# Block-sparse attention and a cosine-routed expert layer on one core: first pair in half transfers, bf16 mask rows, routing sums on GpSimd, early dispatch in 16 steps, x and weights in pieces, PSUM pools of their own

## The chip, the cores and the metric

The kernel runs on one core of a Trainium2 chip. TensorE (PE) does the matmuls, with its weight loads shown as a row of their own (PEld); VectorE (DVE), ScalarE (ACT) and GpSimd (POOL) do the rest, and SyncE (SP) issues most transfers. The metric is the device time of one execution in microseconds, as the median of several. All times below are microseconds unless ns is written.

## The reference

```python
# attention: batch 4, heads 8, 768 tokens, 64 per head, blocks of 32 tokens
scores = scale * q @ k.T                      # per batch and head
mask = |blk_i - blk_j| <= 1, or block 0 or 23 on either side,
       or one of 3 sampled key blocks of the query's block
attn = exp(scores masked to -1e9, less the row's maximum) / (sum + 1e-9)
x = (attn @ v), heads side by side            # 3072 rows of 512
# experts: 8 of them, F = 1024, one per row
logits = normed(x) @ normed(expert_emb).T / tau
expert_idx = argmax(logits); gate = softmax(logits)[expert_idx]
out[row] = gate * (relu(x[row] @ w1[e]) @ w2[e])
```

## The kernel before, in words

**Attention.** Heads are handled in 16 pairs, four pairs to a sequence (a batch item). A pair has two halves of 384 queries, and a half has six key chunks of 128. One half and one chunk is a unit, `u`; 192 units in all, 6 to a half pair, 12 to a pair, 48 to a sequence. `score_fast` adds the mask and the scores of a unit in PSUM: four bf16 matmuls of `kmask` by `qmask` and eight f32 matmul passes of `kt` by `qt`, and ScalarE takes the exp into `e` (four buffers, L300). The mask is a product: `kmask` has a row for each block with ones at its tokens, `qmask` for each block the value (0 or -1e9) that it gives to a query. `attend_fast` multiplies with V into `av` (L318) and adds up `esum` on VectorE (L313, L315); after the sixth chunk ScalarE copies half of `av` out (L322) and VectorE adds the other (L324). `turn_fast` transposes K and Q of the next pair on PE (L280) and copies them out with VectorE (`kt`, L283) and ScalarE (`qt`, L284).

`settle` (called at u % 6 = 3 for the half pair before) turns the result back into rows (L346), sums the denominators (L353), and writes rows of x and parts of the logits (L361, L364). `squares` (u % 6 = 4) squares x and adds up its columns on GpSimd (L375, L379).

**Routing.** `after_sequence` makes a plan of steps for the units that follow a sequence: the four steps of `route` at units 8, 10, 11 and 13 (sum of squares, sum of logit parts, norm and argmax, gate, then x to DRAM), `rank` at 14 (three products on PE, then VectorE), and after the second sequence `dispatch_early` in nine steps at units 16 to 26, which finds five full tiles of 128 rows of one expert; then the transfers for expert tiles 0 and 1 at units 28 and 29 (`fetch`), and `prepare` of tile 0 at 44. x and the weights go in whole transfers of 1.5 MB and 2 MB.

**Experts.** `expert_tile` does 64 f32 matmul passes for the hidden layer in two halves of 32 (`hp`, L685), the transposes of the next tile (L670) and the second layer (`yp`, L698). At tile 0, between the halves, the last half pair is settled and the last sequence routed.

**Order.** The framework orders the instructions of each engine by program order and readiness: an instruction traced late but ready early may be moved forward. `issue_after(ins)` puts what is traced in its block behind `ins`, on that instruction's engine alone and without waiting for its end. Each engine then works in that fixed order. Pools of PSUM lie on a stack: `small` (one tile of two banks, for turn, settle, rank and others), `big_f` (two tiles of two banks, the scores), `acc` (two banks, av); after attention `eps` takes the six banks of the last two.

**Start.** `attention_fast` L726 to L742: ids and the first pair's K on SP and Q on ScalarE's queue, V, the expert table, the second pair, then constants, mask (`build_mask`), expert table, both halves of `turn_fast`, and two `score_fast`.

Of the kernel before, what the change touches and what calls it, by code (L numbers as in the profile page):

```python
# [11 lines left out]
F32 = mybir.dt.float32  # L12
# [45 lines left out]

def build_consts(k):
    nc, pool = k.nc, k.const  # L60
    k.ident = pool.tile([P, P], F32, name="ident")
    make_identity(nc, k.ident[:])
# [35 lines left out]
def build_mask(k):  # L98


    nc, pool = k.nc, k.setup
    ids_f = pool.tile([NB, NRAND], F32, name="ids_f")
    nc.vector.tensor_copy(out=ids_f, in_=k.ids)

# [6 lines left out]
    for val in (0.0, float(NB - 1)):  # L111
        for pos in (col, row):
            nc.vector.scalar_tensor_tensor(out=m, in0=pos, scalar=val, in1=m, op0=ALU.is_equal, op1=ALU.max)
# [3 lines left out]
    nc.vector.tensor_scalar(out=m, in0=m, scalar1=1.0, scalar2=-NEG, op0=ALU.subtract, op1=ALU.mult)  # L117

    oh = pool.tile([P, NC, NB], F32, name="oh_blk")
# [14 lines left out]
    if not k.exact:  # L134
        k.kmask = k.const.tile([P, S], BF16, name="kmask")
        k.qmask = k.const.tile([P, S], BF16, name="qmask")
        nc.gpsimd.memset(k.kmask, 0.0)
        nc.gpsimd.memset(k.qmask, 0.0)
        for h in range(2):
            nc.vector.tensor_copy(out=k.kmask[D * h:D * h + NB, :], in_=krow)  # L140
            nc.scalar.copy(out=k.qmask[D * h:D * h + NB, :], in_=qr[0:NB, 0:S])
        return
# [41 lines left out]
def load_pair(k, g, parts=(0, 1, 2), engine=None):  # L184
    b, j = g // NPAIR, g % NPAIR
    got = k.loaded.setdefault(g, [None, None, None])
    for i in parts:
# [6 lines left out]
        got[i] = t  # L194

# [71 lines left out]
def turn_fast(k, g, part):  # L267
# [6 lines left out]
    for n in range(2):  # L274
        src = k.loaded[g][n]
        for c in range(NQ):
            for r in range(2):
                toks = slice(D * r, D * (r + 1))
                for h in range(2):
                    nc.tensor.matmul(ps[D * h:D * (h + 1), r, n, c, :], lhsT=src[toks, h, part * NQ + c, :],  # L280
                                     rhs=k.ident[toks, toks], start=True, stop=True)
# [46 lines left out]
def settle(k, w):  # L328
# [28 lines left out]
    nc.vector.tensor_scalar(out=den, in0=den, scalar1=1e-9, scalar2=None, op0=ALU.add)  # L357
    inv = k.sp.tile([P, NQ, 2], F32, name="inv", tag="inv")
# [68 lines left out]
def route(k, b):  # L427
# [7 lines left out]
    else:  # L435
        nc.vector.reduce_sum(out=nrm, in_=k.nsq[b], axis=AX.X)
# [7 lines left out]
    if not k.exact:  # L444
        nc.vector.reduce_sum(out=l, in_=k.part[b].rearrange("p c h e -> p c e h"), axis=AX.X)
# [17 lines left out]
    gate = p.tile([P, NC], F32, name="gate")  # L463
    nc.vector.reduce_sum(out=gate, in_=ex, axis=AX.X)
    nc.vector.tensor_scalar(out=gate, in0=gate, scalar1=1e-9, scalar2=None, op0=ALU.add)
    nc.vector.reciprocal(out=x[:, :, DM:XW], in_=gate.unsqueeze(2))
    for dram in (k.x_early, k.x_dram):
        if dram is k.x_dram or b < EARLY:
            nc.sync.dma_start(out=dram[b * S:(b + 1) * S, :].rearrange("(p c) w -> p (c w)", c=NC),
                              in_=x.rearrange("p c w -> p (c w)"))  # L470
    for c in range(NC):
        t = b * NC + c
        nc.gpsimd.tensor_tensor(out=k.seen[:, t + 1, :], in0=k.seen[:, t, :], in1=k.oh[:, t, :], op=ALU.add)
    yield

# [17 lines left out]
def add_up(k, t):  # L493

    for step in (1, 2, 4):
# [3 lines left out]
        t = nxt  # L499
    return t  # L500


def tile_experts(k, end, tiles, name):
# [6 lines left out]
    nc.vector.reduce_sum(out=ex, in_=past, axis=AX.X)  # L510
    nc.vector.tensor_scalar(out=ex, in0=ex, scalar1=float(E - 1), scalar2=None, op0=ALU.min)
# [16 lines left out]
def split_places(k, pos, nt, tiles):  # L528
# [8 lines left out]
    nc.vector.scalar_tensor_tensor(out=low, in0=hi, scalar=-float(G), in1=pos, op0=ALU.mult, op1=ALU.add)  # L537
    nc.vector.tensor_tensor(out=ge[:, :, 0:tiles], in0=ge[:, :, 0:tiles], in1=ge[:, :, 1:tiles + 1], op=ALU.subtract)
# [31 lines left out]
def dispatch_early(k):  # L570
# [8 lines left out]
    end = add_up(k, full)  # L579
    yield  # L580
    nc.vector.tensor_scalar(out=end, in0=end, scalar1=float(NE), scalar2=None, op0=ALU.min)
    k.experts = [tile_experts(k, end, NE, "expert_e")]
# [6 lines left out]
    pos = of_expert(k, base, nt, "pos")  # L589
    late = p.tile([P, nt], F32, name="late")  # L590
    taken = of_expert(k, k.taken, nt, "taken_t")
    nc.vector.tensor_tensor(out=late, in0=k.rank[:, 0:nt], in1=taken, op=ALU.is_ge)
# [3 lines left out]
    low, val = split_places(k, pos, nt, NE)  # L596
# [6 lines left out]
def dispatch_late(k):  # L603
# [9 lines left out]
    end = add_up(k, need)  # L613
    k.used = k.const.tile([P, 1], I32, name="used")
    nc.vector.tensor_scalar(out=k.used, in0=end[:, E - 1:E], scalar1=float(NG), scalar2=None, op0=ALU.min)
    k.experts.append(tile_experts(k, end, NG, "expert_l"))
# [9 lines left out]
    low, val = split_places(k, pos, NT, NG)  # L626
# [15 lines left out]
def fetch(k, i):  # L642
    nc = k.nc
    late = int(i >= NE)
    t = i - NE if late else i
    e = nc.values_load(k.experts[late][0:1, t:t + 1], engines=(mybir.EngineType.SP,), min_val=0, max_val=E - 1)
    wp = k.wp if i % 3 < 2 else k.wp2
    w1 = ring(k, "w1", i, 3, wp, [P, ND, F])
    nc.sync.dma_start(out=w1, in_=k.w1[bass.ds(e, 1), :, :].rearrange("o (c p) f -> p (o c) f", p=P))
    w2 = ring(k, "w2", i, 3, wp, [P, NF, DM])  # L650
    nc.sync.dma_start(out=w2, in_=k.w2[bass.ds(e, 1), :, :].rearrange("o (c p) m -> p (o c) m", p=P))
    x = ring(k, "xg", i, 4, k.wp, [P, XW])
    slot = k.slots[late][:, t:t + 1]
    nc.gpsimd.indirect_dma_start(  # L654
# [4 lines left out]
    k.fetched[i] = (w1, w2, x, slot)  # L659
# [281 lines left out]
```

## Time and profile before

| | us |
|---|---|
| median of 3 runs (779.92 to 782.65) | 780.49 |
| the profiled execution | 785.54 |
| its span, first to last instruction | 783.6 |
| first attention matmul (L318) starts | 20.4 |
| last unit's attention matmul starts | 372.4 |
| first expert matmul (L685) starts | 374.68 |
| one expert tile in the steady stretch | 14.45 |
| mean granted clock | 0.992 |

A row of the profile is start, length, engine, line, operation, result <- operands, count, and in brackets the idle time before it and what ended it. "SPq" is the issuing of a transfer on a queue. "issue" is idle time for which the profile shows no waiting. The stretches give busy time of each engine and, in the last three columns, the granted PE clock (1.00 is full), the share of the DMA engines that was busy, and GB/s.

### The profile page before, as it was taken

The page shows a single profiled execution, that of the slowest core. Times are in us where ns is not written, and L with a number is a line of the kernel's source. Part 1 is how long each engine was busy: PE and PEld are TensorE (multiplying, and loading weights), DVE is VectorE, ACT ScalarE, POOL GpSimd, SP SyncE. Part 2 cuts the span into 40 slices and gives each one's busy share as a digit, 9 for nine tenths or more (in the row PEclk, how much of TensorE's full clock was granted, in tenths as well). Part 3 has the DMA queues.
Part 4 walks back from the last instruction along what each step waited for, and adds up shares of the span by engine and source line. Part 5 has one row for each costly group of instructions (what it writes and reads, how often), then busy time and mean ns, then how long its engine had stood idle before and what let it go on. Part 6 is the DMA issues. An engine that isn't in the chain of part 4 may idle for free.

```text
span 783.6 us, 22560 instructions
## 1 busy us (share of the span) xinstructions
PE 751.3 (96%) x10028; PEld 496.4 (63%) x10028; DVE 329.5 (42%) x645; ACT 201.1 (26%) x298; POOL 199.2 (25%) x354
## 2 busy tenths in 40 slices
PE   5999999999989999999999999999999999999992
PEld 2555555555546655555777677677687786786771
DVE  3666667667786668666481111111111111111110
ACT  2555544554544454455100000000000000000000
POOL 2034443344335345334321121121121111110210
PEclk9999999999999999999999999999999999999997
DMA  4022224311199321200799989989999999899890
GB/s 153 32 63 63 64 63 160 127 59 32 38 293 402 137 63 55 92 3 3 266 374 353 346 304 335 343 286 345 325 307 344 320 326 337 309 335 330 299 334 25
DMA packets 64099, 165.47 MB, mean 211 GB/s; under 512 B 2988, under 2 KB 15276, under 8 KB 63222
## 3 DMA queue, kind: packets, MB, share of 16 engines
q1 hardware_dynamic: 59238, 149.60, 54.8%
q0 software_dynamic: 4480, 13.91, 4.4%
q8 instruction: 82, 1.34, 0.7%
q10 hardware_dynamic: 272, 0.39, 0.2%
q14 instruction: 27, 0.22, 0.1%
HBM read 148.14 MB, written 16.54 MB: 210 GB/s over the span
## 4 chain that ended last, share of the span: by engine, by line
PE 82%; issue 6%; DVE 6%; POOL 2%; DMA 2%; ACT 1%; SPq 0%; POOLq 0%; DVEq 0%; ACTq 0%
PE hp L685 22%; PE yp L698 21%; PE sc L297 17%; PE av L318 14%; PE turn L280 3%; DVE esum L315 2%; PE back L353 2%; PE xg_ps L670 1%; POOL sq L379 1%; PE back L346 1%; ACT e L300 1%; DMA out_dram<-y,slot_l 1%; DMA emb<-in_moe_expert_emb_dram 1%; DVE x L361 1%; PE qr L132 0%
## 5 line engine op out<-in xcount | busy, mean ns | idle before, releaser
L685 PEld LDWEIGHTS hp<-xgt,w 128*128 128x128 f32 x1728 | 198.8, 193 | 13.6 <-issue 11.4
L685 PE MATMUL hp<-xgt,w 128*128 128x128 f32 x1728 | 199.7, 277 | 1.4 <-DVE at L324 1.4
L698 PE MATMUL yp<-w,h 128*128 128x512 f32 x432 | 189.9, 593 | 0.0
L300 ACT ACTIVATE e<-sc 128x768 f32<-128x768 f32 x192 | 155.1, 810 | 124.4 <-PE sc L297 123.8
L318 PE MATMUL av<-e,vld 64*64 64x384 f32 x1536 | 162.4, 490 | 5.6 <-ACT e L300 4.4
L297 PE MATMUL sc<-qt,kt 64*64 64x384 f32 x1536 | 162.9, 486 | 1.7 <-issue 1.6
L315 DVE TENSOR_TENSOR esum<-esum,e 128x768 f32<-128x768 f32 x128 | 134.9, 1054 | 66.8 <-ACT e L300 64.2
L698 PEld LDWEIGHTS yp<-w,h 128*128 128x128 f32 x432 | 80.1, 190 | 90.3 <-issue 90.3
L688 ACT ACTIVATE h<-hp 128x512 f32<-128x512 f32 x27 | 16.1, 597 | 363.6 <-PE hp L685 363.6
L379 POOL TENSOR_TENSOR sq<-sq 128x192 f32<-128x192 f32 (+1 forms) x186 | 91.4, 491 | 13.2
L701 POOL DMA_INDIRECT out_dram<-y,slot_l x22 | 22.0, 1002 | 267.8 <-DVE y L700 255.7
L318 PEld LDWEIGHTS av<-e,vld 64*64 64x64 f32 x1536 | 51.6, 133 | 57.1 <-ACT e L300 30.4
L692 DVE TENSOR_SCALAR h<-hp 128x512 f32<-128x512 f32 x27 | 18.7, 692 | 160.1 <-PE hp L685 159.8
L297 PEld LDWEIGHTS sc<-qt,kt 64*64 64x64 f32 x1536 | 60.3, 134 | 40.3 <-issue 37.7
L700 DVE TENSOR_SCALAR y<-yp,xg 128x512 f32<-128x512 f32 x27 | 20.3, 751 | 154.1 <-PE yp L698 154.0
L375 POOL TENSOR_TENSOR sq<-x 128x384 f32<-128x384 f32 x31 | 26.4, 850 | 209.0 <-DVE part L364 180.4
L297 PE MATMUL sc<-qmask,kmask 64*64 64x384 bf16 x768 | 68.1, 325 | 0.7 <-issue 0.7
L297 PEld LDWEIGHTS <-kmask 64*64 64x64 bf16 x768 | 25.6, 108 | 32.8 <-issue 31.9
L313 DVE TENSOR_TENSOR esum<-e 128x768 f32<-128x768 f32 x32 | 31.0, 970 | 20.4 <-ACT e L300 20.4
L284 ACT ACTIVATE qt<-turn 128x384 f32<-128x384 f32 x32 | 15.7, 490 | 50.5 <-DVE kt L283 50.5
L353 PE MATMUL back<-ones,esum 64*64 64x1 f32 x1536 | 26.6, 191 | 0.0
L654 POOL DMA_INDIRECT xg<-x_dram,slot_l x24 | 24.7, 1028 | 7.4 <-issue 7.4
(159 smaller groups left out, 383.2 us busy)
## 6 DMA issues: line engine op xcount, KB each, us to landing
w<-in_moe_w_dram SPq DMA_DIRECT2D x58, 2048.0 KB, 10.6
x_dram<-x SPq DMA_DIRECT2D x4, 1539.0 KB, 11.5
kld<-in_k_dram SPq DMA_DIRECT2D x16, 384.0 KB, 4.7
vld<-in_v_dram SPq DMA_DIRECT2D x16, 384.0 KB, 3.5
qld<-in_q_dram SPq DMA_DIRECT2D x15, 384.0 KB, 5.2
x_early<-x SPq DMA_DIRECT2D x2, 1539.0 KB, 8.8
qld<-in_q_dram ACTq DMA_DIRECT2D x1, 384.0 KB, 3.3
xg<-x_dram,slot_l POOLq DMA_INDIRECT x24, 7.3
```

Of the source, the lines that this page charges most:

```text
L280: nc.tensor.matmul(ps[D * h:D * (h + 1), r, n, c, :], lhsT=src[toks, h, part * NQ + c, :], rhs=k.ident[toks, toks], start=True, stop=True)
L297: nc.tensor.matmul(ps[D * r:D * (r + 1), h, 0:HALF], lhsT=rows[D * h:D * (h + 1), keys], rhs=cols[D * h:D * (h + 1), queries], start=first ...
L300: k.exps = nc.scalar.activation(e, ps[:, :, 0:HALF], ACT.Exp)
L313: k.summed = nc.vector.tensor_tensor(out=k.esum, in0=k.first, in1=e, op=ALU.add)
L315: k.summed = nc.vector.tensor_tensor(out=k.esum, in0=k.esum, in1=e, op=ALU.add)
L318: nc.tensor.matmul(k.av[D * h:D * (h + 1), r, 0:HALF], lhsT=v[D * r:D * (r + 1), h, kc, :], rhs=e[D * r:D * (r + 1), h, :], start=(kc == 0 ...
L353: nc.tensor.matmul(sums[D * s:D * (s + 1), t, h, r:r + 1], lhsT=esum[D * r:D * (r + 1), h, cols], rhs=k.ones[D * r:D * (r + 1), 0:1], star ...
L375: nc.gpsimd.tensor_tensor(out=sq, in0=x, in1=x, op=ALU.mult)
L379: nc.gpsimd.tensor_tensor(out=out, in0=sq[:, :, 0:width], in1=sq[:, :, width:2 * width], op=ALU.add)
L654: nc.gpsimd.indirect_dma_start(out=x[:, :], out_offset=None, in_=(k.x_dram if late else k.x_early)[:, :], in_offset=bass.IndirectOffsetOnA ...
L685: nc.tensor.matmul(hp[:, f, :], lhsT=w1[:, d, (f0 + f) * P:(f0 + f + 1) * P], rhs=xt[:, d, :], start=(d == 0), stop=(d == ND - 1))
L698: nc.tensor.matmul(yp, lhsT=h[:, f, :], rhs=w2[:, f, :], start=(f == 0), stop=(f == NF - 1))
```

## The change

- **Start.** `load_first` loads K and Q of the first pair as two halves of three chunks each, into separate tiles of the same rings; the ids go behind the first half of K. The identity is built first, then the mask; the first half is turned and scored (two units) before the second half is turned. `build_consts` comes behind the two copies of the mask on VectorE and ScalarE, the second pair and the expert table after it, and `build_experts` at unit 3.
- **Mask.** `kmask` is made in bf16 by a memset and two affine_selects on 64 rows and copied to the other 64; `qmask` comes from two bf16 matmuls of 384 columns, and is copied by VectorE and ScalarE half each. The f32 path is kept for the exact fallback.
- **Routing.** The sums over squares, logit parts and exps are pairwise adds on GpSimd. Steps move to units 7, 10, 11, 12, rank stays at 14, the gate's reciprocal is at 13; x goes in six pieces of 0.26 MB for each destination, from unit 13 on.
- **Early dispatch** in 16 steps at units 16 to 38, every third left out. Rows of tiles 0 and 1 are gathered at units 40 and 41, the weights go in eight pieces of 0.5 MB each: tile 0's at units 27 to 45, tile 1's and `prepare(0)` in the sequence after.
- **Tick.** Each `settle` sends one denominator to DRAM; planned steps on SP come behind it.
- **PSUM.** `acc` lies below `big_f`; `eps` has xg_ps and yp (two banks), a new pool `hps` the four of hp.

```diff
-def build_mask(k):
+def block_mask(k, exact=False):
...
+    ids_f = pool.tile([NB, NRAND], F32, name="ids_f")
+    with k.tc.issue_after(ins.ins):
+        nc.vector.tensor_copy(out=ids_f, in_=k.ids)
     for r in range(NRAND):
...
+    both = pool.tile([NB, 2, D], F32 if exact else BF16, name="both")
...
+    nc.vector.tensor_scalar(out=both[:, :, 0:NB], in0=m.unsqueeze(1).broadcast_to([NB, 2, NB]), scalar1=1.0,
+                            scalar2=-NEG, op0=ALU.subtract, op1=ALU.mult)
+    return both
+def build_mask(k):
...
+    nc.vector.memset(k.kmask[0:D], 1.0)
+    both = block_mask(k)
+    one = k.kmask[0:D].rearrange("p (c t) -> p c t", c=NC)
+    nc.gpsimd.affine_select(out=one, in_=one, pattern=[[1, NC], [NC, P]], compare_op=ALU.is_ge,
+                            fill=0.0, base=0, channel_multiplier=-BLK)
+    nc.gpsimd.affine_select(out=one, in_=one, pattern=[[-1, NC], [-NC, P]], compare_op=ALU.is_ge,
+                            fill=0.0, base=BLK - 1, channel_multiplier=BLK)
+    nc.vector.tensor_copy(out=k.kmask[D:P], in_=k.kmask[0:D])
+    ps = k.big.tile([P, 2, 512], F32, name="qr", tag="big")
+    for i in range(2):
+        cols = slice(i * HALF, (i + 1) * HALF)
+        nc.tensor.matmul(ps[:, i, 0:HALF], lhsT=both.rearrange("p h b -> p (h b)"), rhs=k.kmask[0:NB, cols],
+                         start=True, stop=True)
+    for i, copy in enumerate((nc.vector.tensor_copy, nc.scalar.copy)):
+        cols = slice(i * HALF, (i + 1) * HALF)
+        k.masked.append(copy(out=k.qmask[:, cols], in_=ps[:, i, 0:HALF]).ins)
...
+def load_first(k):
+    k.loaded[0] = [[None, None], [None, None], None]
+    for half in range(2):
+        for n, (name, src, engine) in enumerate((("k", k.k, k.nc.sync), ("q", k.q, k.nc.scalar))):
+            t = k.ld.tile([P, 2, NC, D], F32, name=f"{name}ld", tag=f"{name}ld", bufs=2)[:, :, 0:NQ]
+            engine.dma_start(out=t, in_=src[0, 0:2].rearrange("h (p c) d -> p h c d", c=NC)
+                             [:, :, half * NQ:(half + 1) * NQ, :])
+            k.loaded[0][n][half] = t
+        if half == 0:
+            load_ids(k)
+    load_pair(k, 0, (2,))
...
+    k.tick = nc.sync.dma_start(out=k.ticks[w:w + 1, :], in_=den[0:1, 0:1])
...
-        nc.vector.reduce_sum(out=nrm, in_=k.nsq[b], axis=AX.X)
+        nsq = k.nsq[b]
+        nc.gpsimd.tensor_tensor(out=nsq[:, :, 0:2], in0=nsq[:, :, 0:2], in1=nsq[:, :, 2:4], op=ALU.add)
+        nc.gpsimd.tensor_tensor(out=nrm.unsqueeze(2), in0=nsq[:, :, 0:1], in1=nsq[:, :, 1:2], op=ALU.add)
...
-        nc.vector.reduce_sum(out=l, in_=k.part[b].rearrange("p c h e -> p c e h"), axis=AX.X)
+        part = k.part[b]
+        for w in (4, 2):
+            nc.gpsimd.tensor_tensor(out=part[:, :, 0:w], in0=part[:, :, 0:w], in1=part[:, :, w:2 * w], op=ALU.add)
+        nc.gpsimd.tensor_tensor(out=l, in0=part[:, :, 0], in1=part[:, :, 1], op=ALU.add)
...
     for c in range(NC):
         t = b * NC + c
         nc.gpsimd.tensor_tensor(out=k.seen[:, t + 1, :], in0=k.seen[:, t, :], in1=k.oh[:, t, :], op=ALU.add)
+    for w in (4, 2):
+        nc.gpsimd.tensor_tensor(out=ex[:, :, 0:w], in0=ex[:, :, 0:w], in1=ex[:, :, w:2 * w], op=ALU.add)
+    gate = x[:, :, DM:XW]
+    nc.gpsimd.tensor_tensor(out=gate, in0=ex[:, :, 0:1], in1=ex[:, :, 1:2], op=ALU.add)
+    nc.gpsimd.tensor_scalar(out=gate, in0=gate, scalar1=1e-9, scalar2=None, op0=ALU.add)
+    yield
+    nc.vector.reciprocal(out=gate, in_=gate)
+    drams = (k.x_early, k.x_dram) if b < EARLY else (k.x_dram,)
+    for dram in drams:
+        for c in range(NC):
+            nc.sync.dma_start(out=dram[b * S:(b + 1) * S, :].rearrange("(p c) w -> p c w", c=NC)[:, c], in_=x[:, c])
+            yield
...
+def fetch_weights(k, i, pieces=1):
...
+    for w, src in ((w1, k.w1), (w2, k.w2)):
+        src = src[bass.ds(e, 1), :, :].rearrange("o (c p) f -> p (o c) f", p=P)
+        step = w.shape[1] // pieces
+        for c in range(0, w.shape[1], step):
+            nc.sync.dma_start(out=w[:, c:c + step], in_=src[:, c:c + step])
+            yield
...
-        hp = ring(k, f"hp{f0}", i, 2, k.eps, [P, half, P])
+        hp = ring(k, f"hp{f0}", i, 2, k.hps, [P, half, P])
...
-    plan = [(8, routing), (10, routing), (11, routing), (13, routing), (14, partial(rank, n, b))]
+    plan = [(7, routing), (10, routing), (11, routing), (12, routing), (14, partial(rank, n, b))]
+    plan += [(13, routing)] + [(15 + NC * (i // 4), routing) for i in range(NC * (1 + (b < EARLY)))]
     if b == EARLY - 1:
         step = partial(next, dispatch_early(n), None)
-        plan += [(u, step) for u in (16, 17, 18, 20, 21, 22, 23, 24, 26)]
-        plan += [(28, partial(fetch, n, 0)), (29, partial(fetch, n, 1)), (44, partial(prepare, n, 0))]
+        plan += [(u, step) for u in range(16, 39) if u % 3]
+        plan += [(40, partial(fetch_rows, n, 0)), (41, partial(fetch_rows, n, 1))]
+        step = partial(next, fetch_weights(n, 0, 4), None)
+        plan += [(u, step) for u in (27, 27, 33, 33, 39, 39, 45, 45)]
+    if b == EARLY:
+        step = partial(next, fetch_weights(n, 1, 4), None)
+        plan += [(u, step) for u in (3, 3, 9, 9, 27, 27, 33, 33)]
+        plan += [(44, partial(prepare, n, 0))]
...
-    n.big, n.acc = pool("big_f", 2, space=PSUM), pool("acc", 1, space=PSUM)
+    n.acc, n.big = pool("acc", 1, space=PSUM), pool("big_f", 2, space=PSUM)
...
+    load_first(n)
+    build_ident(n)
+    build_mask(n)
+    turn_fast(n, 0, 0)
+    score_fast(n, 0)
+    score_fast(n, 1)
+    turn_fast(n, 0, 1)
+    with n.tc.issue_after(n.masked[0]), n.tc.issue_after(n.masked[1]):
+        build_consts(n)
+    load_pair(n, 1)
+    load_experts(n)
...
+        if u == 3:
+            with n.tc.issue_after(n.summed.ins), n.tc.issue_after(n.exps.ins):
+                build_experts(n)
+            setup.close()
...
-                with n.tc.issue_after(n.summed.ins), n.tc.issue_after(n.exps.ins):
+                with n.tc.issue_after(n.summed.ins), n.tc.issue_after(n.exps.ins), n.tc.issue_after(n.tick.ins):
                     what()
...
-        n.wp2, n.eps = pool("wp2", 1), pool("eps", 1, space=PSUM)
+        n.wp2, n.eps, n.hps = pool("wp2", 1), pool("eps", 1, space=PSUM), pool("hps", 1, space=PSUM)
```

## The prediction

> **What bounds the kernel now.** I read the page first, then the chain that ended last, who PE waited for, the spacing of a repeating ScalarE copy, and the load by stretches.
>
> ```profile
> PE 751.3 (96%) x10028; PEld 496.4 (63%) x10028; DVE 329.5 (42%) x645; ACT 201.1 (26%) x298; POOL 199.2 (25%) x354
> ```
>
> PE is the bound; PE's useful work is hardly touched by the change, so only time in which PE stands still or runs slowly can be won. The chain, in order of time (start, length, what), opens with:
>
> ```profile
> 2.88 4.82 DMA emb<-in_moe_expert_emb_dram
> 10.13 0.88 DVE krow L129
> 11.05 2.75 PE qr L132 x4
> 13.80 1.53 PE turn L280 x48
> 16.49 1.56 PE turn L280 x48
> 18.05 2.52 PE sc L297 x16
> ```
>
> The first attention matmul (av) starts at 20.4. Before it stand a load of the expert table that attention doesn't need, the f32 mask matmul (2.75) and two transposes in a row. What PE waited for in the whole run (total, times, longest):
>
> ```profile
> PE av L318 <- ACT e L300: 4.4, 5, 1.7
> PE tp L173 <- DVE emb L170: 3.9, 1, 3.9
> PE sc L297 <- issue: 2.3, 3, 1.1
> PE hp L685 <- DVE at L324: 1.4, 1, 1.4
> ```
>
> The copy of L322 comes once per half pair (six units). In quiet stretches its spacing is 10.73; around the end of the second sequence it is not:
>
> ```profile
> 203.45 0.47 ACT L322 COPY part<-av 128x384 f32<-128x384 f32 x1
> ...
> 215.15 0.47 ACT L322 COPY part<-av 128x384 f32<-128x384 f32 x1
> ...
> 228.86 0.48 ACT L322 COPY part<-av 128x384 f32<-128x384 f32 x1 [1.75 <-PE av L318]
> ```
>
> That is 11.70 and 13.71. The surplus over 10.73, from all starts of this copy: 0.97, 1.13, 1.04 after sequence 0 (3.14); 0.97, 2.98, 1.74, 1.52, 0.89 after sequence 1 (8.10), then 0.51 where prepare(0) falls; 0.96, 1.14 after sequence 2 (2.10). In all 13.85. One cause, in the timeline:
>
> ```profile
> 117.67 0.18 DVE L436 TENSOR_REDUCE nrm<-nsq 128x6 f32<-128x24 f32 x1 [0.66 <-POOL nsq L379]
> ...
> 118.23 0.84 DVE L445 TENSOR_REDUCE l<-part 128x48 f32<-128x384 f32 x1
> ```
>
> VectorE waits for GpSimd in order, then reduces, and esum, exp and av come late. By stretches (us, busy PE, PEld, DVE, ACT, POOL, then granted clock, DMA share, GB/s), a quiet half pair, the routing, the early dispatch:
>
> ```profile
> 43.60:54.40 10.80, 10.78 (x248) 6.14 (x244) 7.35 (x13) 5.61 (x8) 4.20 (x8) 1.00 0.12 43
> 119.00:130.00 11.00, 10.06 (x232) 5.97 (x236) 9.39 (x25) 5.74 (x10) 5.37 (x15) 1.00 0.26 87
> 219.00:230.00 11.00, 9.32 (x214) 5.50 (x210) 9.61 (x36) 4.47 (x7) 3.62 (x8) 1.00 1.05 307
> ```
>
> VectorE has 3.4 free in a quiet half pair and some 1.4 in the others; in the last the DMA engines are full too. At the change to the experts the clock halves:
>
> ```profile
> 374.00:376.00 2.00, 1.32 (x9) 1.32 (x10) 0.62 (x3) 0.00 (x0) 1.66 (x3) 0.85 0.79 117
> 376.00:378.00 2.00, 2.00 (x11) 2.00 (x11) 0.00 (x0) 0.00 (x0) 1.29 (x6) 0.50 1.02 416
> ```
>
> From 374.68 the expert tiles run at 14.45 each, 27 of them, PE bound; the change leaves them alone. The profiled execution took 785.54 (span 783.6 and 1.9 around it), 5.05 over the median 780.49. The sum is made on it and taken off the median unchanged.
>
> **The start.** K and Q come in halves. The whole Q alone on ScalarE's queue landed 3.3 after its issue at 0.80; a half should land no later, at 4.1 (bound above: 4.8, what kld took). turn(0,0) 1.53, to 5.6; kt 0.57 and qt 0.50, to 6.7. The ids go behind the first K half, at about 1.3; before, the cast's wait ended 3.56 after the ids' issue, so 4.9 (above: emb's 4.8 behind two loads, so 6.1). Then cast 0.45 at most, three mask steps of 0.25, "both" 0.17: 6.3. GpSimd: ident is done at 1.5, three iotas 0.4, a memset, two affine_selects over 768 columns; L121 took 0.327 for 144 and the identity's 0.287 for 128, so in proportion 1.7 each: 5.5, and VectorE's copy to the other 64 rows some 0.5, within the ids' wait. Two bf16 mask matmuls of 384 columns, 0.325 each by L297's row: 7.0. qmask's copy of 384 columns, 0.56 as kt: 7.6. If kt falls between the mask steps, qt is last instead, at about the same time. Score 0 therefore starts at 7.7 (7.0 to 9.5 with the bounds). From there PE has the eight mask matmuls (1.33 in this trace at that point), 2.6 for 16 score matmuls and turn(0,1) 1.56, so av starts at 13.2: 7.2 earlier.
>
> What was done under the old wait now lies in attention. build_consts: six VectorE steps, about 1.0, and eight GpSimd steps, under VectorE's and GpSimd's slack (5.35 and 0 busy of 10 in the first 10 us of attention). build_experts at unit 3: PE tp 0.59 on the path, VectorE some 2.2 in steps under 0.6, ScalarE 0.8. PE queues in order behind tp, whose chain (ScalarE 0.8, GpSimd 0.58, VectorE 0.8) is 2.2 long; a wait of 0 to 2.2, I take 0.4, since the program interleaves units there. emb is loaded behind the first pair and needed some 10 later; the cover is its early issue, without it ScalarE's exp would stand behind its square. Net gain 6.2 (3.5 to 8.5).
>
> **Routing sums on GpSimd.** Per sequence VectorE loses 0.18, 0.84, 0.19 and 0.17 to 0.49: 1.5, and the wait of 0.66 for GpSimd. GpSimd gains two adds of 0.2, adds of 192, 96 and 48 columns (1.08, 0.41, 0.33 by the squares' rows, L379), and 0.24, 0.64, 0.25, 0.2 for the gate: 3.6. It is busy 4.2 of 10.73, so this fits; the first sums go a unit earlier, the second step stays at unit 10, leaving three units (4.4) for 0.4 of norm adds, the power (1.35) and 1.8 of logit adds. Behind VectorE's second step and its reciprocal are queued esum and so e's four buffers: a late GpSimd shows there. *A page against this:* the Trainium skill, "GPSIMD Engine Reference", section 4.1 Engine selection, gives free-axis sums to VectorE and calls two-input work on GpSimd about twice as slow. The rows agree on the price (0.84 against 1.08 + 0.41 + 0.33). If the work were on the path, four sequences would lose 4 x 2.1 = 8.4 and the saving would shrink to 8; I go by the idle share of GpSimd instead.
>
> **Early dispatch and pieces.** The nine steps over units 16 to 26 hold some 9 of VectorE time; as 16 steps over 16 to 38 (3.8 half pairs) they are 2.4 each against 3.4 free. The 3 MB of x and the 8 MB of two weight sets, issued within about 9 us, filled the DMA from 219 to 257; PE's 1.1 and 0.5 of "issue" at 235 and 242 lie in it, another at 138 under x. In pieces behind the tick, DMA carries some 1.6 to 2.7 MB per half pair (0.6 of loads, 1 of x, 1 of weights), 150 to 250 GB/s where rows up to 428 stand. 32 ticks (0.25 of SP each, the zero row's price) hold SP until the denominators are there; queued behind are the K, Q and V loads, issued 25 before their use (40.4 for a turn at about 66), so nothing is late. 30 more x issues of 0.37 go to SP, which is idle. The two row gathers move 12 units back (1.2 to 1.7 of GpSimd each), far ahead of prepare(0), now one sequence later. In the last sequence six x issues stand before tile 3's weights: 2.2 of SP against over 10 of lead.
>
> What stays: rank's PE work 0.76 three times, slot 0.39, prepare 0.51: 3.2. Over the eleven half pairs touched I leave 0.3 each for esum meeting a step or GpSimd's port (esum is 0.96 alone and 1.39 to 1.62 beside the first squares): 3.3. So 13.85 becomes 6.5, a gain of 7.3. Bounds: 10.6 if only PE's work stays, minus 5 if GpSimd's queue is late each time (below).
>
> **Own PSUM pools.** L685's first matmul waits 1.43 for L324, the last reader of av. With hp on the banks of the scores it waits for the last exp, long done when av leaves PE: 1.43. The first 32 matmuls took 5.47, half a tile's 7.14 is 3.57: 1.9 through the clock of 0.50. The nearest cause in the trace is that pause; without it I take 1.6 of the 1.9. *A rule that disagrees:* "TensorE: Matmul & The Clock Gate", Part 1, wants an idle window of about 3.4 us for the drop; here 1.43 idle and a thin 2 us before it were followed by 0.50. By the rule the 1.9 isn't the pause's and this part would be 1.4. Gain 3.0 (0 to 3.3). Last routing: VectorE waits for GpSimd's sums in front of h's second half, which was done 1.3 before yp needed it; I take 0, at worst -2.
>
> Sum: 6.2 + 7.3 + 3.0 = 16.5; 785.5 becomes 769.0, the median 764.0.
>
> **Rivals.** (1) GpSimd's queue is late. Squares of the last half pair (4.6) stand in front of seen and the gate; VectorE's reciprocal or PE's rank waits. For: L379 ran 1.08 instead of 0.6 for 192 columns, and PE already waited at rank. Against: 6 of 10.73 free. Boundary gain gone: 780.5 - 9.2 = 771. (2) The start gives little: ids or masks at their bounds plus the full tp wait and a slow clock; 2 instead of 6.2: 768; gone altogether, 770. (3) Slower: the same GpSimd queue, but with PE's rank matmuls ordered in front of ready units, so that each of three boundaries waits the whole 4.6 + 3.6 = 8.2, less the 1.5 saved, 6.7 x 3 = 20 in place of the gain of 7.3: 780.5 - 9.2 + 20 = 791. It decides from 3.1 per boundary on. Against it: a unit lies between seen's step and rank's. (4) It does nothing: waits return elsewhere (pools still released together, masks late): 778 to 782.
>
> **Chances.** Forecast 0.66 (own range 757 to 769), (1) 0.12, (2) 0.09, (3) 0.07, (4) 0.06. To leave 2 in 10 out, the range goes to 774 above and 756 below. 0.5%, some 4 us, is what a measurement can tell here: faster 0.86 (all of the first three but 0.01), same 0.06, slower 0.08.
>
> **What would show it.** First av at 12 to 15; no f32 qr; spacing of L322's copy at most 11.4 at the boundaries with VectorE not waiting for GpSimd's nsq; no DMA share of 1.0 from 200 to 260; hp starting within 0.3 of av's end and 1.00 granted there. Wrong if PE waits for POOL or for "both", or if the copies keep 11.7 and more.

## The result, and the profile after

The changed kernel takes 791.57 (median; 790.0 to 792.01) beside 781.13 for the kernel before: a ratio of 1.0129, with a 95% interval of 1.0105 to 1.0153. The change makes the kernel 10 slower; the forecast was 764.0. Its profiled span is 790.1, and 783.6 before.

Line numbers moved: av is now L360 (L318 before), the copy out of av L364 (L322), VectorE's half of it, `at`, L366 (L324), the gate's sums L516 to L519, its reciprocal L521, hp L769 (L685).

PE is busy as long as before, so the time is again one in which PE stands still or runs slowly:

```profile
PE 752.5 (95%) x10020; PEld 493.2 (62%) x10020; DVE 324.6 (41%) x629; ACT 200.4 (25%) x297; POOL 214.6 (27%) x388
```

The copy that comes once per half pair shows where. Around the end of the first sequence:

```profile
122.56 0.47 ACT L364 COPY part<-av 128x384 f32<-128x384 f32 x1
141.78 0.47 ACT L364 COPY part<-av 128x384 f32<-128x384 f32 x1
152.51 0.47 ACT L364 COPY part<-av 128x384 f32<-128x384 f32 x1
```

19.22 and then the quiet 10.73 again. The same half pair after the second and third sequence takes 18.18 (217.13 to 235.31) and 18.53 (311.99 to 330.52). The half pair in front of each takes 10.97, where it was 11.70, and of the four behind the second boundary none is over 11.30, where 12.47 and 12.25 stood. So nearly all the surplus over 10.73, 23.7 of 25.8, now lies in three half pairs.

The list of waits of the whole run (total, times, longest) names the two engines in front of PE:

```profile
PE av L360 <- DVE at L366: 15.8, 4, 5.2
...
DVE x L521 <- POOL x L519: 12.3, 4, 3.9
...
DVE nrm L496 <- POOL nrm L483: 5.9, 4, 2.1
...
PE tp L201 <- DVE emb L198: 2.0, 1, 2.0
```

In the timeline of the first slow half pair, the chain is complete:

```profile
122.42 0.83 POOL L419 TENSOR_TENSOR sq<-x 128x384 f32<-128x384 f32 x1 [3.22 <-DVE x L405]
...
122.49 1.58 DVE L357 TENSOR_TENSOR esum<-esum,e 128x768 f32<-128x768 f32 x1
...
123.22 0.91 POOL L514 TENSOR_TENSOR seen<-seen,oh 128x8 f32<-128x8 f32 x1
...
124.64 0.20 POOL L514 TENSOR_TENSOR seen<-seen,oh 128x8 f32<-128x8 f32 x1
...
126.83 0.52 POOL L516 TENSOR_TENSOR ex_l<-ex_l 128x24 f32<-128x24 f32 x2
...
127.72 0.26 POOL L519 TENSOR_SCALAR x<-x 128x6 f32<-128x6 f32 x1
128.02 0.20 DVE L521 RECIPROCAL x<-x 128x6 f32<-128x6 f32 x1 [3.95 <-POOL x L519]
128.13 0.52 DVE L366 TENSOR_TENSOR at<-av,part 128x384 f32<-128x384 f32 x1
...
128.70 1.56 PE L360 MATMUL av<-e,vld 64*64 64x384 f32 x8 [4.90 <-DVE at L366]
```

GpSimd works almost without a gap from 122.42 to 127.98: the squares of the half pair just settled, the six `seen` adds between them, then the gate's sums, last. That half pair is the first of the next sequence, so the gate stands behind work that it doesn't need. VectorE has come to the gate's reciprocal at 124.07 and stands there for 3.95. Next in its order is `at`, 0.52 long and with nothing of its own missing. `at` is the last reader of av's only PSUM buffer, so PE stands for 4.90. And PE doesn't come back at full speed. By stretches (length, busy PE, PEld, DVE, ACT, POOL; then granted clock, DMA share, GB/s):

```profile
125.00:127.00 2.00, 0.00 (x0) 0.00 (x0) 0.00 (x0) 0.00 (x0) 1.92 (x11) 1.00 0.05 16
127.00:129.00 2.00, 0.30 (x4) 0.30 (x8) 0.98 (x3) 0.00 (x0) 0.74 (x4) 0.65 0.00 0
129.00:131.00 2.00, 2.00 (x18) 0.69 (x13) 0.98 (x2) 0.49 (x1) 0.00 (x0) 0.50 0.84 224
131.00:133.00 2.00, 2.00 (x20) 0.77 (x16) 0.17 (x1) 0.81 (x1) 0.00 (x0) 0.50 0.89 287
133.00:135.00 2.00, 2.00 (x20) 0.83 (x12) 0.78 (x1) 0.21 (x1) 0.00 (x0) 0.64 0.04 14
```

At 0.50, 0.50 and 0.64, the six microseconds from 129 cost 2.7 more. 4.90 and 2.7 are 7.6 of the 8.49 over the quiet half pair.

At the start, the first av is where the prediction put it (12.44 for 13.2), 7.9 earlier than before. But the first copy of L364 is at 25.70, only 2.9 before the old 28.61. `build_experts`, now at unit 3, took the rest:

```profile
18.06 0.61 ACT L194 ACTIVATE emb_sq<-emb 8x512 f32<-8x512 f32 x1
...
18.85 0.75 POOL L195 TENSOR_TENSOR emb_nrm<-emb_nrm,half 8x1 f32<-8x1 f32 x1 [14.34 <-ACT emb_sq L194]
...
20.11 0.47 DVE L198 TENSOR_SCALAR emb<-emb,emb_nrm 8x512 f32<-8x512 f32 x1
...
20.64 0.41 PE L201 MATMUL tp<-ident,emb 8*128 8x8 f32 x4 [1.98 <-DVE emb L198]
```

PE waits in order for a chain over three engines, and the clock is 0.95, 0.50 and 0.70 in the three stretches of 2 us from 20 on (1.7 lost).

In this execution the change to the experts went as forecast: PE goes from av to hp without a pause and at full clock, where 1.43 of pause and 0.50 stood in the profile of before; the first 32 matmuls take 3.84, not 5.47.

```profile
382.19 0.86 PE L360 MATMUL av<-e,vld 64*64 64x384 f32 x8
382.98 3.84 PE L769 MATMUL hp<-xgt,w 128*128 128x128 f32 x32
```

### The profile page after: what moved, and what is told of

Read it like the earlier page. It is cut to its first block, busy times and chain, and to the rows that moved or that the text cites. A ratio compares the mean times of both kernels' runs of the same rounds, so it can differ in the third digit from the quotient of the medians.

```text
span 790.1 us, 22711 instructions
## 1 busy us (share of the span) xinstructions
PE 752.5 (95%) x10020; PEld 493.2 (62%) x10020; DVE 324.6 (41%) x629; ACT 200.4 (25%) x297; POOL 214.6 (27%) x388
## 4 chain that ended last, share of the span: by engine, by line
PE 83%; issue 5%; POOL 4%; DVE 3%; DMA 2%; ACT 1%; SPq 0%; POOLq 0%; DVEq 0%; ACTq 0%
PE hp L769 22%; PE yp L782 21%; PE sc L339 18%; PE av L360 15%; PE back L395 2%; PE turn L322 2%; PE xg_ps L754 1%; PE back L388 1%; ACT e L342 1%; DMA out_dram<-y,slot_l 1%; POOL sq L423 1%; DVE esum L357 1%; DMA vld<-in_v_dram 1%; POOL nrm L483 1%; DMA ids<-in_sampled_blocks_dram 0%
## 5 line engine op out<-in xcount | busy, mean ns | idle before, releaser
L769 PEld LDWEIGHTS hp<-xgt,w 128*128 128x128 f32 x1728 | 197.1, 192 | 12.1 <-issue 11.5
L769 PE MATMUL hp<-xgt,w 128*128 128x128 f32 x1728 | 198.1, 275 | 0.0
L360 PE MATMUL av<-e,vld 64*64 64x384 f32 x1536 | 167.6, 501 | 16.5 <-DVE at L366 15.8
L339 PE MATMUL sc<-qt,kt 64*64 64x384 f32 x1536 | 165.8, 495 | 0.1
L360 PEld LDWEIGHTS av<-e,vld 64*64 64x64 f32 x1536 | 51.6, 136 | 70.6 <-ACT e L342 25.4
L423 POOL TENSOR_TENSOR sq<-sq 128x192 f32<-128x192 f32 (+1 forms) x186 | 89.7, 482 | 12.5
L322 PEld LDWEIGHTS turn<-ident,kld 64*64 64x64 f32 x768 | 17.9, 137 | 14.9 <-issue 5.8
```

The lines of the kernel that those rows point to most:

```text
L339: nc.tensor.matmul(ps[D * r:D * (r + 1), h, 0:HALF], lhsT=rows[D * h:D * (h + 1), keys], rhs=cols[D * h:D * (h + 1), queries], start=first ...
L360: nc.tensor.matmul(k.av[D * h:D * (h + 1), r, 0:HALF], lhsT=v[D * r:D * (r + 1), h, kc, :], rhs=e[D * r:D * (r + 1), h, :], start=(kc == 0 ...
L423: nc.gpsimd.tensor_tensor(out=out, in0=sq[:, :, 0:width], in1=sq[:, :, width:2 * width], op=ALU.add)
L769: nc.tensor.matmul(hp[:, f, :], lhsT=w1[:, d, (f0 + f) * P:(f0 + f + 1) * P], rhs=xt[:, d, :], start=(d == 0), stop=(d == ND - 1))
```

## The experiments

**Theory A**: the loss is the gate's reciprocal at step 13, which holds VectorE in order until GpSimd is through; PE behind it, and then the clock. **Theory B**: the sums on GpSimd are the loss in themselves, wherever the reciprocal stands. Each kernel below is the changed kernel but for its edit, where nothing else is said. Ratios are to the kernel before, with 95% intervals.

**1. The reciprocal later (recip_late).**

```diff
-    plan += [(13, routing)] + [(15 + NC * (i // 4), routing) ...]
+    plan += [(17, routing)] + [(21 + NC * (i // 4), routing) ...]
```

> Only the gate's reciprocal on VectorE (L521) and the x pieces behind it move, four to six units later; all GpSimd sums stay. Theory A (one VectorE instruction that waits for GpSimd stands in front of the copy-out of av, L366, and PE's pause then halves the clock): the three long half pairs (19.22, 18.18, 18.53) fall to 12 or less, the time to 771 (767 to 775). Theory B (GpSimd has too much to do after a sequence, wherever its results are awaited): the wait turns up at the next place, and the time stays above 784.

Measured: 775.47, ratio 0.9919 [0.9896, 0.9941]: just over A's 775, far under B's 784. Two numbers in the plan turn 1.3% slower into 0.8% faster. GpSimd's gate is done no earlier in its own order, but VectorE comes to the reciprocal two microseconds after it, and no idle time stands in front of it:

```profile
127.71 0.91 POOL L519 TENSOR_SCALAR x<-x 128x6 f32<-128x6 f32 x1
...
130.62 0.18 DVE L521 RECIPROCAL x<-x 128x6 f32<-128x6 f32 x1
```

The three half pairs take 12.31, 12.57 and 12.52 (A had at most 12): 18.5 less in all. The spans account for it: 18.5, plus 1.4 at the first copy, where PE's same wait of 1.98 for `tp` was followed here by no drop of the clock, less 3.1 for one half pair that is now 14.34 and was 11.22 (experiment 6), give 16.8; 790.1 to 773.4 is 16.7.

**2. The sums alone on the kernel before (sums_only).** Norm, logit and gate sums on GpSimd as in the change, with `seen` in front of the gate's sums as there, steps 7, 10, 11, 12 and 13; nothing else of it.

```diff
-    plan = [(8, routing), (10, routing), (11, routing), (13, routing), (14, partial(rank, n, b))]
+    plan = [(7, routing), (10, routing), (11, routing), (12, routing), (13, routing), (14, partial(rank, n, b))]
-        nc.vector.reduce_sum(out=nrm, in_=k.nsq[b], axis=AX.X)
+        nc.gpsimd.tensor_tensor(out=nsq[:, :, 0:2], in0=nsq[:, :, 0:2], in1=nsq[:, :, 2:4], op=ALU.add)
...
```

> The kernel before with only the norm, logit and gate sums on GpSimd, at the steps of after (7, 10, 11, 12, reciprocal at 13). Theory A (the reciprocal at step 13 waits for GpSimd in front of at, and the rest of the change has no part in it): each of three boundaries gets a half pair of 18 to 19.5 in place of 11.7 to 13.7, so 780.5 + 3 x 6.5 = 800, 795 to 804. Rival E (the wait needs the pieces and the early dispatch as well): 780 to 786.

Measured: 798.9, ratio 1.0228 [1.0211, 1.0245]; half pairs of 18.13, 19.18 and 19.34; VectorE's wait for the gate 12.2 over four times, PE's for `at` 16.7 over five. The part does the whole harm alone, and the rest of the change is worth some 7 beside it (798.9 to 791.6).

**3. The reciprocal one unit later (recip14).**

```diff
-    plan += [(13, routing)] + [(15 + NC * (i // 4), routing) ...]
+    plan += [(14, routing)] + [(21 + NC * (i // 4), routing) ...]
```

> The gate's reciprocal goes one unit later (step 14, not 13), the x pieces as in recip_late. In VectorE's order it then stands behind the add of the last scores' output (at) and the first esum, in front of the second esum; GpSimd's gate sum ends no earlier, so VectorE still waits some 4 us. Theory A (what costs is that av waits for at, which stood behind the reciprocal): av has its free bank, esum has four buffers of e as slack, so PE waits under 3 us and at most part of the clock drop is left: 776 to 782, the three half pairs at 12.3 to 15. Rival C (any wait of 4 us on VectorE costs the same, wherever it stands, since VectorE has only some 1.5 us free per half pair there): 788 to 792, half pairs over 17.

Measured: 791.54, ratio 1.0121 [1.0089, 1.0152]: as slow as the change. The half pairs take 16.56, 16.81 and 20.03, all over A's 15, two of them a little under C's 17. Theory A was too narrow: it isn't `at` alone that matters, but whatever comes next on VectorE. Behind the reciprocal there is now the copy of K, which PE's scores wait for:

```profile
130.02 0.19 DVE L521 RECIPROCAL x<-x 128x6 f32<-128x6 f32 x1 [3.26 <-POOL x L519]
130.12 0.52 DVE L325 COPY kt<-turn 128x384 f32<-128x384 f32 x1
...
130.70 0.88 PE L339 MATMUL sc<-qt,kt 64*64 64x384 f32 x8 [2.35 <-DVE kt L325]
```

PE waits less than in the change: 7.0 over three times for `kt`, and 3.3 for `at` that recip_late has too, where the change has 15.8. The clock takes the rest: over recip_late's half pairs the three have 4.25, 4.24 and 7.51 more, nearly all of it the pause of 2.35 each and then 1.7, 1.7 and 5.1 of slow clock. After the third boundary's wait of 2.35 it stays down for ten microseconds:

```profile
320.00:322.00 2.00, 2.00 (x18) 1.60 (x14) 1.23 (x3) 1.38 (x2) 0.00 (x0) 0.60 0.33 118
322.00:324.00 2.00, 2.00 (x20) 0.77 (x16) 1.08 (x3) 0.00 (x0) 0.00 (x0) 0.50 0.00 0
324.00:326.00 2.00, 2.00 (x61) 1.61 (x56) 0.24 (x1) 0.81 (x1) 0.00 (x0) 0.50 0.00 0
```

(0.50 until 330, then 0.84.) After the waits of the first and second boundary, of the same 2.35, it was 0.67, 0.50, 0.98 and 0.71, 0.50, 0.94.

So rival C holds only in part: the three half pairs are 2.5 shorter in sum than the change's, and the time is equal because the half pair of experiment 6 takes 14.36, as in recip_late, where the change has 11.22, and the first copy came 1.1 later. The x pieces stand here where recip_late has them, so it isn't their move that helped in recip_late.

**4. Which sums are worth moving (gate_dve, norm_dve, all_dve).** gate_dve takes the gate's sum back to VectorE and leaves norm and logits on GpSimd; norm_dve does the opposite; all_dve takes all three back, at steps 8, 10, 11, 12 and 13.

```diff
-    gate = x[:, :, DM:XW]
-    nc.gpsimd.tensor_tensor(out=gate, in0=ex[:, :, 0:1], in1=ex[:, :, 1:2], op=ALU.add)
...
+    nc.vector.reduce_sum(out=gate, in_=ex, axis=AX.X)
```

> The gate's sum goes back to VectorE at the step where its reciprocal is; the sums of squares and logit parts stay on GpSimd. Theory A: VectorE no longer waits for GpSimd in front of L366; half pairs at the boundaries at most 12, time 771 (767 to 776). Theory B: GpSimd still has the squares, seen and 2.7 us of other sums in a row; the time stays above 784.

> The sums of squares and of logit parts go back to VectorE, the gate's sum stays on GpSimd with its reciprocal where it was. Theory A: the gate's place is untouched, so the three long half pairs stay near 18 to 19 and the time at 791 (788 to 794). Theory B: with 2.7 us less on GpSimd per sequence the wait shrinks and the time falls under 785.

> Everything of the change but the sums: norm, logit and gate sums on VectorE at the steps of before (8, 10, 11, 13). By theory A (the sums are a gain once nothing waits for the last of them) this is slower than recip_late by the 1.5 us of VectorE and the wait for GpSimd's nsq per boundary: 777 to 782, boundaries at 12 to 14. Rival D (GpSimd's sums were worth nothing or harmful in themselves): 770 to 775, at or below recip_late.

Measured: gate_dve 777.16, 0.9936 [0.9916, 0.9957]; norm_dve 799.54, 1.022 [1.0197, 1.0243]; all_dve 773.94, 0.9913 [0.9896, 0.9929]. Without a wait for the gate most of the loss is gone; gate_dve's three half pairs are still 13.14 to 13.43 (theory A: 12) and its time 1 over A's range. norm_dve, 5.5 over A's range, keeps that wait (14.8 over four times) and adds one of 2.5 at each boundary for GpSimd's squares, since the norm's sum now stood on VectorE a unit too early; I read it at first as proof that moving these sums was a gain. all_dve, with the norm's step at 8, shows that it isn't: its two half pairs at the first boundary take 11.70 and 11.85, where recip_late has 10.97 and 12.31, and over three boundaries the two kernels differ by 0.3 (70.0 and 70.3). Rival D holds, within 0.5%: moving the sums brought nothing, even with nobody waiting for the last one. The wait of 0.66 for GpSimd's squares that the move removed has come back as one of up to 2.1 for its power (L496, 5.9 over four times in the list of waits of after).

**5. build_experts in two steps (experts_split).** Its norm at unit 3, its transposes and copies at unit 7.

```diff
-        if u == 3:
+        if u in (3, 7):
...
-                build_experts(n)
+                next(experts)
```

> The transposes and copies of the expert table come at unit 7 instead of 3, its norm stays at unit 3. Theory C (PE waits 2.0 in order for the table at unit 3, and then runs at half clock): the first copy of av (L364) moves from 25.7 to about 21.7, the time falls by 4 to 787.5 (786 to 790). Rival: VectorE's and ScalarE's own 3 us for the table delay attention wherever they stand; 791.

Measured: 790.79, ratio 1.0112 [1.009, 1.0134]. The first copy comes at 21.27 in place of 25.70, PE waits 0.2 in front of `tp`, the clock is 1.00 from 18 to 32. The next half pair gives back 1.1 (11.83), in which the steps of unit 7 lie, and one half pair much later takes 13.06 in place of 11.22. Of the 4.4 there are 2.5 left in the span, and 0.8 between the medians. So theory C was right about the wait and the first copy, but its 786 to 790 was missed: the time is the rival's 791. The first copy also varies by itself: it comes at 24.31 to 26.79 in the six kernels that keep the change's start, and at 20.50 to 23.24 in the four that split it.

**6. Putting it together (best, best2, best3).** best has recip_late's idea and experts_split, the routing's VectorE steps one unit later and the weights in other units; best2 leaves the routing as in recip_late and moves all early weights under the last sequence:

```diff
-        plan += [(u, step) for u in (27, 27, 33, 33, 39, 39, 45, 45)]      # b == EARLY - 1
-        plan += [(u, step) for u in (3, 3, 9, 9, 27, 27, 33, 33)]          # b == EARLY
+        plan += [(u, first) for u in (3, 3, 3, 3, 9, 9, 9, 9)]             # b == EARLY
+        plan += [(u, step) for u in (15, 15, 33, 33, 39, 39, 45, 45)]
```

best3 is best2 with the sums of all_dve.

> recip_late and experts_split together, with the routing's VectorE steps one unit later (11, 12, 13, rank 15, reciprocal 18), so that VectorE's norm step finds GpSimd's power done, and the weights of the first two tiles spread from two sequences' early half pairs to later ones. From recip_late's 775.5: 3.0 to 4.4 at the start, some 0.8 at each of three boundaries, 3 at the half pair of 14.3: 765 to 770. Rival: the slots only move the same VectorE work, and the half pair of 14.3 was not the weights': 771 to 774.

> recip_late (routing steps unchanged at 7, 10, 11, 12, rank 14, reciprocal 17) with build_experts in two steps, and the weights of the first two tiles loaded wholly under the last sequence, so that in the half pair of 14.3 us the x pieces, K, Q, V and the row gathers are alone. Theory W (ScalarE's and PE's waits there, which nothing in the trace explains, go with a DMA share near 1.0): that half pair falls to 11.2 to 11.8, the start gains 2 to 3; 775.5 - 2.5 - 2.8 = 770, 768 to 772. Rival (those waits come of the row gathers, not of the weights): 772 to 774.

> The same with the norm, logit and gate sums back on VectorE (all_dve's steps). In all_dve the two half pairs at a boundary took 11.70 and 11.53 to 11.85, in recip_late 10.97 and 12.31 to 12.57: the same sum. If GpSimd's sums are worth nothing (theory D), it lies within 1.5 us of best2: 768 to 772. If they still were a gain (theory A's remainder): 772 to 776.

best measured 775.17, 0.9925 [0.9909, 0.9942]: no better than recip_late, and slower than both its own range and the rival's. The half pairs at its boundaries grew to 13.56 to 13.81, in part since PE's rank now waited for VectorE (2.4 over three times), and one half pair still took 13.12. In that one, the engines stand without a wait that the trace can name, while the DMA engines are full:

```profile
260.00:262.00 2.00, 2.00 (x75) 1.44 (x68) 1.31 (x5) 0.81 (x2) 1.17 (x1) 1.00 0.93 275
262.00:264.00 2.00, 1.82 (x43) 1.21 (x41) 1.40 (x4) 0.22 (x1) 1.70 (x2) 1.00 1.02 363
264.00:266.00 2.00, 2.00 (x32) 1.21 (x28) 1.51 (x3) 0.81 (x1) 1.39 (x3) 1.00 0.97 324
```

```profile
262.24 0.43 PE L397 MATMUL back<-ones,esum 64*64 64x1 f32 x16 [0.18 <-issue]
...
264.18 0.56 DVE L407 TENSOR_TENSOR x<-back,inv 128x384 f32<-128x384 f32 x1 [0.46 <-issue]
...
265.16 0.96 DVE L359 TENSOR_TENSOR esum<-esum,e 128x768 f32<-128x768 f32 x1 [0.31 <-issue]
```

best2, with no weights there, in the same place of the program:

```profile
259.00:261.00 2.00, 2.00 (x51) 1.26 (x51) 1.92 (x5) 0.81 (x1) 0.56 (x1) 1.00 0.70 248
261.00:263.00 2.00, 2.00 (x86) 1.51 (x80) 1.11 (x3) 0.81 (x1) 1.70 (x2) 1.00 0.19 36
```

That half pair is 11.22. The time is the 770 that theory W forecast, and without these loads the half pair is 1.9 to 3.1 shorter than in best and recip_late. But full DMA engines alone don't explain it. The change has the loads there too and takes 11.22, while experts_split and norm_dve, with its transfers and its waits at the boundary, take 13.06 and 13.12; why the change escapes stays open. What the engines lacked isn't named by the trace. Late instructions are one reading: from 258 to 268 best has two packets on the queues that the profile calls "instruction". But best2, where nothing stands, has three from 258 to 266. The Trainium skill, "Runtime: NRT & Kernel Launch", section Instruction fetch mechanics, says that a sequencer fetches its instructions through a DMA queue of its own and that the cost of going on to the next block is mostly hidden. Whether that holds under a DMA share of 0.9 and more no run here shows; none ties a packet to a wait.

best2 measured 770.5, ratio 0.9863 [0.9846, 0.988], best3 770.94, 0.9873 [0.9855, 0.9891]. Both beat the kernel before, by 1.4% and 1.3%, and the change, by 2.7% and 2.6%; their difference says once more that the place of the sums is worth nothing.

**7. The PSUM pools alone on the kernel before (pools_only).**

```diff
-    n.big, n.acc = pool("big_f", 2, space=PSUM), pool("acc", 1, space=PSUM)
+    n.acc, n.big = pool("acc", 1, space=PSUM), pool("big_f", 2, space=PSUM)
...
-        hp = ring(k, f"hp{f0}", i, 2, k.eps, [P, half, P])
+        hp = ring(k, f"hp{f0}", i, 2, k.hps, [P, half, P])
```

> The kernel before with only the PSUM pools of the change (hp on banks of its own, the pools opened in the other order). The prediction's step: 1.43 of pause and 1.6 of clock, 780.5 - 3.0 = 777.5, 776.5 to 778.5, first 32 hp matmuls at 3.6 to 4.0. Rival (the clock's drop has another cause): 1.4 alone, 779.

Measured: 779.22 beside 780.6, ratio 0.9979 [0.997, 0.9989]: 1.6, between 0.9 and 2.3. That is the rival's 779 (the pause of 1.4 alone), not the 3.0 of the prediction's step. In the profiled execution there is no pause, and the first 32 matmuls take 3.84 at full clock.

```profile
369.78 0.85 PE L318 MATMUL av<-e,vld 64*64 64x384 f32 x8
370.57 3.84 PE L685 MATMUL hp<-xgt,w 128*128 128x128 f32 x32
```

```profile
370.00:372.00 2.00, 2.00 (x20) 1.44 (x13) 1.83 (x7) 0.48 (x1) 0.94 (x3) 1.00 0.24 41
372.00:374.00 2.00, 2.00 (x20) 2.00 (x19) 0.00 (x0) 0.00 (x0) 1.69 (x5) 1.00 0.82 254
```

From its last copy of av to the end it takes 407.2, the profiled execution of before 410.3: 3.1. The medians show half of that, and sums_only points to why. It has the pools of before and the same pause of 1.43 in the same place, and there the 32 matmuls take 3.84 too, at a granted clock of 1.00:

```profile
390.05 3.84 PE L693 MATMUL hp<-xgt,w 128*128 128x128 f32 x32 [1.43 <-DVE at L324]
```

From its last copy to the end it takes 408.4. So both executions with the old pools have the pause, and one of them the slow clock behind it; how often others have it isn't known.

## Why the prediction was wrong

The forecast was a span of 767.1 (783.6 less 16.5). The change's is 790.1, 23.0 more. All starts of the copy say where: the surplus over the half pairs touched was to be 6.5 and is 25.8 (19.3); the start gained 2.9, not 6.2 (3.3); the last half pair, into which `prepare(0)` moved, took 10.75 where it took 10.00 (0.75); the end gained 3.3, not 3.0.

- **The step that failed** is "It is busy 4.2 of 10.73, so this fits", said of GpSimd. The price of the gate's adds was about right (1.33, and they took 1.15); the others were dearer (0.89 for 0.4, and 2.35 for 1.8, means of four sequences). But a share of idle time says nothing about when the last result is there. The reciprocal stood two units behind the step that makes `oh`; in that time lay GpSimd's squares, which can't start before the next sequence's first x, then `seen`, then the gate: 5.6 in one queue (122.42 to 127.98), against the 1.6 that VectorE needed to get there (122.49 to 124.07). Both numbers could be had from the trace of before, and what stands behind the reciprocal too:

```profile
127.08 0.20 DVE L466 RECIPROCAL x<-gate 128x6 f32<-128x6 f32 x1
127.18 0.52 DVE L324 TENSOR_TENSOR at<-av,part 128x384 f32<-128x384 f32 x1
...
129.72 0.19 POOL L379 TENSOR_TENSOR nsq<-sq 128x3 f32<-128x3 f32 x1
```

GpSimd's last square ends 2.8 after VectorE has come to the reciprocal, and the gate's adds were to stand behind it. The prediction named what is queued behind the reciprocal, "esum and so e's four buffers", and took the slack of esum for that of all that follows; `at` stood there, with no slack, and with the step one unit later `kt` (experiment 3).
- **The rivals.** Rival (1) had the place: the squares "stand in front of seen and the gate; VectorE's reciprocal or PE's rank waits". It was given 0.12 and priced as no more than the gain of 7.3 lost, 771; the half pairs touched lost 12.0 (25.8 for 13.85). Rival (3), given 0.07, had a loss of that order, "the whole 4.6 + 3.6" three times, but the wrong engine, PE's rank: no wait of rank for GpSimd is in the list, nor is there one in that of before, where rank's weight loads waited 1.8 for ScalarE. That its 791 is the measured time is luck: its 20 stands for 12.0, its gain of 9.2 at the start and the end for 6.2, and the profiled execution of before lay some 4 over its median. Per boundary the loss came out as 4.9 to 5.2 of pause and the rest mostly clock, where the rival had 6.7 net of pause alone.
- **The saving on VectorE** for which the sums were moved did not exist: all_dve and recip_late are alike. "1.5, and the wait of 0.66" was paid back in the wait for the power (5.9 over four times; all_dve has 1.1): it took 2.13 beside VectorE's adds, not 1.35. The page of the Trainium skill that the prediction weighed and set aside ("GPSIMD Engine Reference", section 4.1 Engine selection) gives such sums to VectorE; the runs put the two engines level here.
- **The start.** First av, no f32 `qr`, the ids: as forecast, though PE waited 1.3 for `both`, which the prediction had named as a sign of being wrong. The failed term is `build_experts`, "a wait of 0 to 2.2, I take 0.4": it was 1.98, and a slow clock of 1.7 behind it had no term at all. A chain of ScalarE, GpSimd and VectorE in front of an operation that PE takes in order has to be priced at its length unless a later place for PE's part is fixed; experiment 5 fixed one, and the wait was 0.2.
- **Early dispatch and pieces** fit what was said of them: 12.47, 12.25 and 11.62 became 10.81, 10.92 and 11.30, and the 11.77 under x became 10.73. But pools_only, with the dispatch and the transfers of before, has 10.93, 11.22 and 12.04 in the first three places (and 12.16 in the last), so how much of this is the change's isn't shown. "DMA carries some 1.6 to 2.7 MB per half pair ... 150 to 250 GB/s" hid one stretch at 0.9 to 1.02 of share; it came into view as soon as the pauses were gone (13 to 14.3, experiment 6).
- **Own PSUM pools**: of the 3.0, the 1.43 of pause was right; the 1.6 of clock was in the profile but not in the times, which show 0.9 to 2.3 in all (experiment 7). The 1.4 that the prediction would have had by the page's rule was nearer.
- **Clock.** The rule that the prediction set against the row (the Trainium skill, "TensorE: Matmul & The Clock Gate", Part 1, an idle window of about 3.4 us) doesn't hold as a limit on one pause here: 2.35 idle was followed by 0.50 three times out of three (experiment 3; PE had also stood for 0.8 to 1.05, 2.5 before each), and 1.43 in the profile of before. The prediction's own reading, that the pause of 1.43 brings the slow clock, doesn't hold either: in sums_only it doesn't. Nor is it a matter of length alone: 1.98 in front of `tp` gave 0.50 in the change and three more kernels, and 1.00 in recip_late and norm_dve. That the page's window runs free of the program's start would fit such a scatter; no run here shows the window.
- **The base.** 16.5 was made on an execution 5.05 over the median and taken off the median unchanged. best2 is the change without its faults: its span is 13.3 under that profile, its median 10.1 under before's. Part of what the profile showed to be won was that execution's own: the slow clock at the experts, and some 2.5 of the 13.85 around the sequence ends, where pools_only has 11.34.

## What to carry to other kernels

Before a step moves to an idle engine, write down for its last result two times: when it can be there, with all that stands in that engine's queue, and when the consumer comes to it in its own order; an idle share answers neither. Then read what stands behind the consumer: the first instruction there with no slack sets the price, and each pause of TensorE of a few microseconds can cost as much again in clock. If the time to spare can't be shown, put the consumer some units later; here four units were worth 2%.

## What the runs showed of the hardware that was not expected

- After a pause of 2.35, TensorE ran at or near half clock for some 4 us at one boundary (0.67, then 0.50) and for 10 at another of the same execution (recip14). After one of 1.43 it ran at 0.50 in the profile of before and at 1.00 in sums_only.
- GpSimd's 8-column add took 0.91 when it started inside VectorE's 1.58 long add of 768 columns, and ended with it, and 0.20 outside it (first timeline above). The Trainium skill, "SBUF — State Buffer", section Who interferes with whom, states that a VectorE instruction with two inputs in SBUF contends with a GpSimd instruction that reads SBUF, and that the ports they share are locked exclusively; these rows agree.
- The two affine_selects over 768 bf16 columns took 0.86 each, half of the 1.7 that the prediction had scaled up from f32 rows of 144 and 128 columns.
